# Counting hand-over times in a kernel's own scheduler, and a plain second layer for one group in eight: channel attention with a GELU feed-forward on Trainium2

## The chip, the cores and the metric

The kernel runs on one core of one Trainium2 chip. The metric is the device time of one execution in microseconds. Before the change it is 2224.11 us in the median of three runs (2223.18 to 2227.49). The engines are called as in the profile: PE multiplies matrices, DVE (vector) and ACT (scalar) work on elements, SP issues the DMAs. POOL has next to nothing to do here.

## The reference

Four batches of q, k and v, each of 6080 tokens by 256 channels, go through an attention over channels (a 256 x 256 matrix per batch), and the result, read as 24320 rows of 256, through a feed-forward layer with 2048 hidden units.

```python
def _attn_ref(q, k, v, tau):                      # B, N, C = 4, 6080, 256
    qn = q / (np.linalg.norm(q, axis=1, keepdims=True) + 1e-06)
    kn = k / (np.linalg.norm(k, axis=1, keepdims=True) + 1e-06)
    s = kn.transpose(0, 2, 1) @ qn / tau
    s = s - s.max(-1, keepdims=True)
    a = np.exp(s)
    a /= a.sum(-1, keepdims=True) + 1e-09
    return v @ a

def _moe_ref(x, w_in, w_out):                     # x: 24320 x 256
    h = x @ w_in                                  # 256 x 2048
    g = 0.5 * h * (1.0 + erf(h / np.sqrt(2.0)))
    return g @ w_out                              # 2048 x 256
```

## The kernel before

**Precision.** Every fp32 operand of a matmul is split into a high part, rounded to the chip's fp32r type, and the rest. A product is three matmuls: low weight by high data, high by high, high weight by low data. So every block that PE reads must first be made twice: its high part on ACT ("hi"), its rest on DVE ("lo", the block minus its high part).

**Two layers.** The attention matrix of a batch is multiplied into w_in, so that per token two layers remain: 256 to 2048 with the gelu, and 2048 to 256. The tokens of a batch are cut into 12 chunks (10 and 11 are a little narrower), the hidden units into four groups g. A **step** (b, c, g) is one group for one chunk; there are 184 of them after a first pair of chunks that is done in another way. A chunk is two halves of up to 256 columns.

**Layer 1 of a step** multiplies blocks 2 x 2 with seven products instead of eight (`ORDER`, `do` in `chunk_ops`, matmul lines L841 to L843). Each product is six matmuls of 256 columns, so a step has 42. They go into PSUM tiles: "one" and "two" (`pa` and `pb`, which swap roles at each step), "x" (`px`) and "z" (`pz`). Between them ACT copies "one" to `px` (x_copy, L847) and "two" to SBUF (p5_copy, L851), and DVE adds: z_add (L855) makes `pz` from "one" and p5, and p5_add (L858) makes p5. The next product into "one" must wait for z_add, which reads it.

**Between the layers** a gelu is taken of four blocks, B22 (from px), B11 (from p5), B21 (from pz) and B12 (from "one"). For B22, B11 and B21, ACT makes hi (L871) and the whole fp32 value in `gs` (L868), and DVE the lo (L874, out `los`). B12 is made whole alone.

**Layer 2 of a step** is crossed as well: seven products (`CROSS`, L973 to L975) with B22, B11, B21 and four blocks T1 to T4 of differences. These take a chain of their own over two engines: DVE makes t_add(0) (L881, 1024 columns), t_add(1) (L883) and t_add(2) (L885) in place in `gs`; ACT rounds T1 and T3 (first t_hi, L888) and, once t_add(2) is done, T2 and T4 (second t_hi, L888); DVE makes the rests (first and second t_lo, L892). The products with T blocks are the fourth to seventh of the seven. A crossed second layer has 42 matmuls of 256 columns and adds up in four PSUM tiles po0 to po3, which a join on DVE (L1009 to L1021) and copies on ACT (L999) put together per chunk and store.

**The plain form** of layer 2 exists too (L957 to L959). It takes B22, B21, B12 and B11 themselves with the blocks of w_out, in 8 products of three matmuls of 512 columns, and no T block. It then needs the hi (L871) and lo (L874) of B12, and only po0 and po1. `plain_out` says where it is used: in chunk (0, 2) and, through `MIXED`, in the last group of chunk (3, 11).

**What else runs in the steps.** The seven (or eight) products of layer 2 of one step are woven between the seven of layer 1 of the next, so the T blocks of a step are made while PE works at the next one. At batches 0 to 2 the scores of the next batch are multiplied in bursts (L416, L418) with splits (L404, L408) and a sum (L429); near the end of a batch come its softmax and the products with w_in. For each chunk the V data of the next one is summed and split (L756 to L760, L773, L777), with the most of it in the first steps (g = 0) of a chunk. The parts of w_out come from HBM for each step (`wo<-keep_out`, four buffers).

**What sets the order.** The program is recorded as a plan, and then `Order.schedule` puts the instructions of ACT, DVE and SP in an order (PE keeps the recorded one). It walks through time with costs from `cost`. Each instruction has a latest time, counted back from PE's instructions by `delay`, and a ready time, counted forward by the same `delay`; among those that are ready the one with the earliest latest time goes first. The order is then fixed by dependencies.

Of the kernel before, what the change touches and what calls it, by code (L numbers as in the profile page):

```python
# [55 lines left out]
PE, ACT, DVE, SP = (mybir.EngineType.PE, mybir.EngineType.Activation, mybir.EngineType.DVE, mybir.EngineType.SP)  # L56
# [22 lines left out]
class Order:  # L79
# [32 lines left out]
    def cost(self, ins, reads, writes):  # L112
        n = max([x[3] for x in reads + writes] + [1])
        psum = any(x[0][0] in ("pa", "pb", "px", "pz", "po0", "po1", "po2", "po3") for x in reads)
        if ins.engine == PE:
            k = reads[0][3] if reads else 1
            if ins.ins[0].dtype == F32:
                return (max(1.69 * k, 112.0),) * 2
            return .4427 * k + 3.4 + 1.5 * (k <= H), .4427 * k + 170
        if ins.engine == DVE:  # L120
            t = n / .96 + 66
            if type(ins).__name__ == "InstTensorCopy" and not psum:
                t = n / 1.92 + 66
            return t, t + 90
        if ins.engine == ACT:
            t = .855 * n + (38 if psum else 70)
            return t + 90 * (len(ins.outs) > 1), t + 105
        return 60, n * 512 / BANDWIDTH

# [48 lines left out]
    def schedule(self, todo, preds, costs):  # L178
        import heapq
        n = len(todo)  # L180
        succs = [[] for _ in range(n)]
        for b, ps in enumerate(preds):
            for a in ps:
                succs[a].append(b)

        def delay(a, b):
            if (a, b) in self.rings:
                return 0
            same = todo[a].engine == todo[b].engine
            if todo[a].engine == SP:  # L190
                return costs[a][1] + DMA_LATE
            return costs[a][0] if same and todo[a].engine == PE else costs[a][1]

        t, nominal = 0.0, {}
        for at in range(n):
            if todo[at].engine == PE:
                nominal[at] = t
                t += costs[at][0]
        late = [0.0] * n
        for a in reversed(range(n)):  # L200
            x = nominal.get(a, t + 1e4)
            for b in succs[a]:
                x = min(x, late[b] - delay(a, b))
            late[a] = x
        left = [len(p) for p in preds]
        ready = [0.0] * n
        engines = (PE, ACT, DVE, SP)
        known = {e: [] for e in engines}
        for at in range(n):
            if not left[at]:  # L210
                known[todo[at].engine].append(at)
        free = {e: 0.0 for e in engines}
        order, now, slip = [], 0.0, 0.0
        dma = 0.0
        events = [0.0]
        while len(order) < n:
            now = heapq.heappop(events)
            while events and events[0] <= now:
                heapq.heappop(events)
            for e in engines:  # L220
                if free[e] > now or not known[e]:
                    continue
                cands = sorted((late[a], a) for a in known[e] if ready[a] <= now)
                soon = [a for a in known[e] if ready[a] > now]
                pick = None
                for l, a in cands:
                    end = now + costs[a][0]
                    if any(late[u] < l and ready[u] < end and max(late[u] + slip, ready[u]) < end for u in soon):
                        continue
                    pick = a  # L230
                    break
                if pick is None:
                    if soon:
                        heapq.heappush(events, min(ready[u] for u in soon))
                    continue
                a = pick
                known[e].remove(a)
                order.append(a)
                free[e] = now + costs[a][0]
                heapq.heappush(events, free[e])  # L240
                if a in nominal:
                    slip = now - nominal[a]
                if e == SP:
                    dma = max(dma, now + DMA_LAT / 2) + costs[a][1]
                for b in succs[a]:
                    ready[b] = max(ready[b], dma + DMA_LAT / 2 if e == SP and (a, b) not in self.rings else now + delay(a, b))
                    left[b] -= 1
                    if not left[b]:
                        known[todo[b].engine].append(b)
                        heapq.heappush(events, max(now, ready[b]))  # L250
        return order

BANDWIDTH, DMA_LAT, DMA_LATE = 320.0, 2000, 6000


def MIXED(b, c):
    return (b, c) == (3, 11)


NARROWS = (4, 9)
# [15 lines left out]
def channel_attention_gelu_ffn(ctx, tc, qk, kqt, vt, tau, w_in, w_out, out):  # L278
# [228 lines left out]
    def plain_out(b, c, g):  # L507
        return (b, c) == (0, 2) or (MIXED(b, c) and g == NWG - 1)
# [907 lines left out]
```

## Time and profile before

| | |
|---|---|
| median of three runs | 2224.11 us |
| the profiled execution | 2226.17 us, its span 2224.4 us |
| granted TensorE clock | 0.997 |
| first step (0,2,0) begins | 161.4 us into the span |
| first step of batch 3 begins | 1711.3 us |
| last step begins | 2204.7 us |
| DMA | 510 MB, 229 GB/s in the mean |

One row of the list of waits names the engine and line that waited, what it waited for, the sum of the time, how often, and the longest. A row of the timeline gives the start in us, the duration, the engine, line and operation, what it writes and reads with their sizes, and in brackets the idle time of the engine ahead of it if that was over 0.15 us. In a list of groups the columns are line, engine, operation, operands, count, then busy time in us and mean duration in ns, then the idle time ahead of them and what ended it. Matmuls overlap: a row shows 0.28 us for a matmul of 256 columns, but the next one starts 0.12 us later. The distance between starts is what one costs. "PEld" is the loading of weights, which runs beside the matmuls.

### The profile page before, as it was taken

To read this page: it belongs to the slowest core of one execution; us is meant where nothing else is said; L and a number is where in the kernel's file an instruction comes from. 1 tells how busy PE (TensorE), PEld (TensorE's weight loads), DVE (VectorE), ACT (ScalarE), POOL (GpSimd) and SP (SyncE) were. 2 spreads that over 40 slices of the span, in tenths; PEclk is the share of its full clock that TensorE was granted. 3 is DMA by queue.
4 is the path that set the end of the run, shared out by engine and by line. 5 is a ranking of instruction groups with operands and counts; after the bars stand their busy time and mean duration, and the time that the engine had idled before them with its cause. 6 is when DMAs were issued, how large, how long until landed. Compare 5 with 4: busy or idle time off the path is not lost.

```text
span 2224.4 us, 42491 instructions
## 1 busy us (share of the span) xinstructions
PE 2159.6 (97%) x16750; PEld 2062.0 (93%) x16750; DVE 2016.1 (91%) x2908; ACT 1691.7 (76%) x2806; POOL 1.3 (0%) x8
## 2 busy tenths in 40 slices
PE   8999999999999999999899999999999999999999
PEld 7788999999999999999899999999999999999998
DVE  6987899999999899999899999999989989889897
ACT  5656788888888878887777777777778777777776
POOL 0000000000000000000000000000000000000000
PEclk9999999999999999999999999999999999999999
DMA  9547787777877777777576666665556656656655
GB/s 378 180 124 278 252 275 245 272 273 241 286 254 268 266 257 257 254 268 237 162 236 226 232 212 208 230 233 193 195 184 220 205 181 216 200 187 209 204 194 179
DMA packets 164360, 510.03 MB, mean 229 GB/s; under 512 B 16832, under 2 KB 27072, under 8 KB 162112
## 3 DMA queue, kind: packets, MB, share of 16 engines
q1 hardware_dynamic: 164160, 507.32, 67.7%
q8 instruction: 131, 2.15, 0.4%
q14 instruction: 69, 0.57, 0.1%
HBM read 469.76 MB, written 37.49 MB: 228 GB/s over the span
## 4 chain that ended last, share of the span: by engine, by line
DVE 35%; PE 29%; ACT 27%; issue 6%; DMA 4%; SPq 0%; DVEq 0%; ACTq 0%
DVE los L892 12%; ACT his L888 8%; ACT gs L868 8%; ACT his L871 5%; DVE gs L881 4%; PE po L975 4%; DVE pz L855 3%; DVE los L874 3%; PE po L973 3%; PE po L974 3%; DVE gs L885 3%; DVE gs L883 3%; DVE vlo L777 2%; DMA out<-osb 2%; PE pa L841 2%
## 5 line engine op out<-in xcount | busy, mean ns | idle before, releaser
L975 PE MATMUL po<-los,wo 128*128 128x256 f32 (+1 forms) x2506 | 711.9, 284 | 23.9 <-DVE los L892 19.3
L973 PE MATMUL po<-his,wo 128*128 128x256 f32 (+1 forms) x2506 | 698.9, 279 | 1.8 <-ACT his L888 0.8
L974 PE MATMUL po<-his,wo 128*128 128x256 f32 (+1 forms) x2506 | 697.3, 278 | 0.0
L975 PEld LDWEIGHTS po<-los,wo 128*128 128x128 f32 x2506 | 470.9, 188 | 48.2 <-DVE los L892 42.8
L892 DVE TENSOR_TENSOR los<-gs,his 128x1024 fp32r<-128x1024 f32 (+1 forms) x358 | 434.3, 1213 | 70.2 <-ACT his L888 64.3
L888 ACT CAST his<-gs 128x1024 fp32r<-128x1024 f32 (+1 forms) x358 | 373.4, 1043 | 162.8 <-DVE gs L885 137.2
L973 PEld LDWEIGHTS po<-his,wo 128*128 128x128 f32 x2506 | 471.1, 188 | 7.5 <-ACT his L888 1.2
L974 PEld LDWEIGHTS po<-his,wo 128*128 128x128 f32 x2506 | 470.9, 188 | 1.0
L874 DVE TENSOR_TENSOR los<-gs,his 128x512 fp32r<-128x512 f32 (+1 forms) x557 | 378.0, 683 | 60.3 <-ACT gs L868 46.0
L841 PE MATMUL pa<-vhi,wl 128*128 128x256 f32 (+1 forms) x920 | 266.0, 289 | 12.7 <-DVE pz L855 10.5
L841 PE MATMUL pb<-vhi,wl 128*128 128x256 f32 (+1 forms) x920 | 263.5, 286 | 5.3 <-ACT gs L868 4.1
L843 PE MATMUL pa<-vlo,wh 128*128 128x256 f32 (+1 forms) x920 | 257.0, 279 | 1.4 <-DVE vlo L777 1.4
L842 PE MATMUL pb<-vhi,wh 128*128 128x256 f32 (+1 forms) x920 | 256.2, 279 | 0.0
L843 PE MATMUL pb<-vlo,wh 128*128 128x256 f32 (+1 forms) x920 | 256.1, 278 | 0.0
L842 PE MATMUL pa<-vhi,wh 128*128 128x256 f32 (+1 forms) x920 | 256.0, 278 | 0.0
L881 DVE TENSOR_TENSOR gs<-gs 128x1024 f32<-128x1024 f32 (+1 forms) x179 | 217.0, 1212 | 23.2 <-ACT gs L868 16.2
L841 PEld LDWEIGHTS pa<-vhi,wl 128*128 128x128 f32 x920 | 172.9, 188 | 24.3 <-DVE pz L855 17.2
L871 ACT ACTIVATE his<-px 128x512 fp32r<-128x512 f32 (+1 forms) x184 | 108.7, 591 | 110.0 <-PE px L843 109.3
L868 ACT ACTIVATE gs<-px 128x512 f32<-128x512 f32 (+1 forms) x184 | 109.3, 594 | 107.4 <-DVE los L892 107.0
L841 PEld LDWEIGHTS pb<-vhi,wl 128*128 128x128 f32 x920 | 173.0, 188 | 11.9 <-ACT gs L868 5.3
L843 PEld LDWEIGHTS pa<-vlo,wh 128*128 128x128 f32 x920 | 172.9, 188 | 2.8 <-DVE vlo L777 2.4
L842 PEld LDWEIGHTS pb<-vhi,wh 128*128 128x128 f32 x920 | 173.3, 188 | 0.4
(286 smaller groups left out, 4637.3 us busy)
## 6 DMA issues: line engine op xcount, KB each, us to landing
wo<-keep_out SPq DMA_DIRECT2D x547, 512.0 KB, 4.3
raw<-qk SPq DMA_DIRECT2D x95, 512.0 KB, 5.9
wo<-keep_out SPq DMA_DIRECT2D x179, 256.0 KB, 3.9
kqc<-kqt SPq DMA_DIRECT2D x72, 512.0 KB, 5.0
v_raw<-vt SPq DMA_DIRECT2D x20, 1024.0 KB, 7.7
out<-osb SPq DMA_DIRECT2D x40, 512.0 KB, 4.7
win<-keep_in SPq DMA_DIRECT2D x12, 1024.0 KB, 7.3
keep_in<-win SPq DMA_DIRECT2D x4, 1024.0 KB, 4.6
```

The lines of the kernel that those rows point to most:

```text
L841: nc.tensor.matmul(o, wls[g][:, a, q], vh[:, at, :h], start=start, stop=False, skip_group_check=True)
L842: nc.tensor.matmul(o, whs[g][:, a, q], vh[:, at, :h], start=False, stop=False, skip_group_check=True)
L843: nc.tensor.matmul(o, whs[g][:, a, q], vl[:, at, :h], start=False, stop=stop, skip_group_check=True)
L868: nc.scalar.activation(out=whole(name), in_=t[SOURCE[name]], func=AF.Gelu)
L871: nc.scalar.activation(out=slot(name)[0], in_=t[SOURCE[name]], func=AF.Gelu)
L874: tt(out=slot(name)[1], in0=whole(name), in1=f32(slot(name)[0]), op=ALU.subtract)
L881: tt(out=g4[:, 0:2], in0=g4[:, 1:3], in1=g4[:, 0:2], op=ALU.subtract)
L888: nc.scalar.copy(out=views[1][:, 2 - 2 * i:4 - 2 * i], in_=views[0][:, 2 * i:2 * i + 2])
L892: tt(out=views[2][:, at], in0=views[0][:, 2 * i:2 * i + 2], in1=f32(views[1][:, at]), op=ALU.subtract)
L973: nc.tensor.matmul(o, w[:, 1, q], mh, start=starts and q == 0, stop=False, skip_group_check=True)
L974: nc.tensor.matmul(o, w[:, 0, q], mh, start=False, stop=False, skip_group_check=True)
L975: nc.tensor.matmul(o, w[:, 0, q], ml, start=False, stop=stops and q == 1, skip_group_check=True)
```

## The change

It has two parts. `MIXED` now holds for the odd chunks of batches 0 to 2: in their fourth group (g = 3) layer 2 is plain. Since batch 0 has its steps from chunk 2 on, these are 5 + 6 + 6 = 17 steps. And the scheduler's `delay` now adds a hand-over time to a producer's latency: `WAIT` of the consumer's engine between two engines, 60 ns more where the consumer waits for more than one source, and 33 ns between two dependent instructions of one engine; ACT's cost is 10 ns higher.

```diff
         if ins.engine == ACT:
-            t = .855 * n + (38 if psum else 70)
+            t = .855 * n + (48 if psum else 80)
             return t + 90 * (len(ins.outs) > 1), t + 105
...
+        sources = [len({todo[a].engine for a in p if todo[a].engine != PE or todo[b].engine != PE}) for b, p in enumerate(preds)]
+
         def delay(a, b):
             if (a, b) in self.rings:
                 return 0
             same = todo[a].engine == todo[b].engine
             if todo[a].engine == SP:
                 return costs[a][1] + DMA_LATE
-            return costs[a][0] if same and todo[a].engine == PE else costs[a][1]
+            if same:
+                return costs[a][0] if todo[a].engine == PE else costs[a][1] + 33
+            return costs[a][1] + WAIT[todo[b].engine] + 60 * (sources[b] > 1)
...
+WAIT = {PE: 58, ACT: 34, DVE: 40, SP: 0}
...
 def MIXED(b, c):
-    return (b, c) == (3, 11)
+    return b < 3 and c % 2 or (b, c) == (3, 11)
```

The lines of the changed kernel from there on are five higher: L881 is L886 in it.

What the scheduler makes of it is seen on DVE in an ordinary step of batch 3, (3,6,2), which has no plain part; p_... is the p5 tile. Before, from p5_add to the second t_lo:

```order
L858 TENSOR_TENSOR p_23169<-pa,p_23169 128x512
L874 TENSOR_TENSOR los<-gs,his 128x512 x2
L881 TENSOR_TENSOR gs<-gs 128x1024
L874 TENSOR_TENSOR los<-gs,his 128x512
L892 TENSOR_TENSOR los<-gs,his 128x1024
L883 TENSOR_TENSOR gs<-gs 128x512
L855 TENSOR_TENSOR pz<-pb,p_23289 128x512
L885 TENSOR_TENSOR gs<-gs 128x512
L1015 TENSOR_TENSOR osb<-osb 128x512
L892 TENSOR_TENSOR los<-gs,his 128x1024
```

And of the change, the same stretch:

```order
L863 TENSOR_TENSOR p_22693<-pa,p_22693 128x512
L879 TENSOR_TENSOR los<-gs,his 128x512 x2
L1020 TENSOR_TENSOR osb<-osb 128x512
L886 TENSOR_TENSOR gs<-gs 128x1024
L879 TENSOR_TENSOR los<-gs,his 128x512
L888 TENSOR_TENSOR gs<-gs 128x512
L897 TENSOR_TENSOR los<-gs,his 128x1024
L890 TENSOR_TENSOR gs<-gs 128x512
L860 TENSOR_TENSOR pz<-pb,p_22813 128x512
L1022 TENSOR_TENSOR osb<-osb 128x256
L897 TENSOR_TENSOR los<-gs,his 128x1024
```

t_add(1) now stands ahead of the first t_lo, t_add(2) ahead of z_add, and a part of the join ahead of t_add(0).

ACT in the same step, from x_copy to the last gelu; before:

```order
L847 COPY px<-pa 128x512
L888 CAST his<-gs 128x1024
L851 COPY p_23169<-pb 128x512
L871 ACTIVATE his<-px 128x512
L888 CAST his<-gs 128x1024
L868 ACTIVATE gs<-px 128x512
L871 ACTIVATE his<-p_23169 128x512
L868 ACTIVATE gs<-p_23169 128x512
L868 ACTIVATE gs<-pa 128x512
L871 ACTIVATE his<-pz 128x512
L868 ACTIVATE gs<-pz 128x512
```

And of the change:

```order
L852 COPY px<-pa 128x512
L893 CAST his<-gs 128x1024
L856 COPY p_22693<-pb 128x512
L893 CAST his<-gs 128x1024
L876 ACTIVATE his<-px 128x512
L873 ACTIVATE gs<-px 128x512
L876 ACTIVATE his<-p_22693 128x512
L873 ACTIVATE gs<-p_22693 128x512
L876 ACTIVATE his<-pz 128x512
L873 ACTIVATE gs<-pa 128x512
L873 ACTIVATE gs<-pz 128x512
```

The second t_hi goes ahead of the gelu of B22, and the whole gelu of B12 (from `pa`) behind the his of B21.

In a plain step, (2,7,3), DVE has this from p5_add to the one of the next step in place of 14 rows with t_add and t_lo:

```order
L863 TENSOR_TENSOR p_17202<-pb,p_17202 128x512
L879 TENSOR_TENSOR los<-gs,his 128x512
L782 TENSOR_TENSOR vlo<-v_raw,vhi 128x256
L879 TENSOR_TENSOR los<-gs,his 128x512
L782 TENSOR_TENSOR vlo<-vs,vhi 128x512
L782 TENSOR_TENSOR vlo<-v_raw,vhi 128x512
L879 TENSOR_TENSOR los<-gs,his 128x512 x2
L1014 TENSOR_TENSOR osb<-osb 128x256
L1016 TENSOR_TENSOR osb<-osb 128x512
L413 TENSOR_TENSOR hl<-raw,hl 128x1024
L860 TENSOR_TENSOR pz<-pa,p_17334 128x512
L413 TENSOR_TENSOR hl<-raw,hl 128x1024
```

The T work of 17 steps is gone; a fourth los (B12) and the start of the chunk's join stand there. In all DVE loses 17 of each t_add and 34 t_lo, and gains 17 los; ACT loses 34 t_hi and 17 copies and gains 17 his.

## The prediction

> **What bounds the kernel now.** I read the page's busy shares first, then the list of waits, then the chain of waits for one stretch of the last batch, then single matmul starts.
>
> ```profile
> PE 2159.6 (97%) x16750; PEld 2062.0 (93%) x16750; DVE 2016.1 (91%) x2908; ACT 1691.7 (76%) x2806; POOL 1.3 (0%) x8
> ...
> DVE 35%; PE 29%; ACT 27%; issue 6%; DMA 4%; SPq 0%; DVEq 0%; ACTq 0%
> ```
>
> The first line alone says "PE". The second, the engine shares of the chain that ended last, says that for 62% of the span the last thing that somebody waited for was on DVE or ACT. So PE is nearly full, but something else sets its pace in many places. The places are in the waits (engine and line, what it waited for, total us, times, longest):
>
> ```profile
> PEld po L975 <- DVE los L892: 42.8, 109, 1.0
> PEld pa L841 <- DVE pz L855: 17.2, 30, 1.4
> ```
>
> ```profile
> ACT his L888 <- DVE gs L885: 137.2, 108, 3.1
> ```
>
> PE waits for the second t_lo (L892) above all, then for z_add (L855). Behind t_lo stands t_hi (L888), which waits for the second difference t_add(2) (L885). And ACT's whole gelu (L868) waits for t_lo in its turn, since it overwrites the gs block that t_lo reads. That closes a circle, and the chain of waits in batch 3, step (3,6,2), shows it (start, duration, what ended last; the longest pieces, the whole gelus between the rows being left out):
>
> ```profile
> 1985.60 1.24 DVE los L892
> 1987.46 0.64 ACT his L871
> 1988.64 0.70 DVE los L874
> 1989.44 1.24 DVE gs L881
> 1990.70 1.06 ACT his L888
> 1991.78 0.97 DVE los L892
> 1992.92 0.69 DVE gs L883
> 1993.61 0.61 DVE pz L855
> 1994.22 0.60 DVE gs L885
> 1994.84 1.06 ACT his L888
> 1995.93 1.24 DVE los L892
> 1997.79 0.63 ACT his L871
> ```
>
> From ACT's his of B11 to the next one (1987.46 to 1997.79) are 10.33 us, and no matmul is in it. In words: gelus of B11, its los, t_add(0), t_hi, t_lo, t_add(1), z_add, t_add(2), the second t_hi and t_lo, the next step's whole gelu of B22 (behind t_lo, from 1997.17 to 1997.79), and again. Against that stands PE's own need, from matmul starts:
>
> ```profile
> 1994.65 0.28 PE L841 MATMUL pa<-vhi,wl 128*128 128x256 f32 x1
> ...
> 1996.89 0.28 PE L974 MATMUL po<-his,wo 128*128 128x256 f32 x1
> 1997.21 0.39 PE L975 MATMUL po<-los,wo 128*128 128x256 f32 x1
> ```
>
> From the first row to the second are 19 matmuls of 256 columns and 2.24 us, 0.1175 to 0.118 each, so a crossed step (42 for layer 1, 42 for layer 2) needs 9.85 to 9.9; I count with 9.85. The step lasts as long as the circle, 10.33, because the L975 that reads the T2 block starts 0.32 after its predecessor, 0.04 behind the end of t_lo (1995.93 + 1.24): 0.48 us a step are lost.
>
> How much is lost in all follows from the first matmul of a stage and that of the next:
>
> ```profile
> 161.43 0.28 PE L841 MATMUL pa<-vhi,wl 128*128 128x256 f32 x1
> ...
> 1711.31 0.28 PE L841 MATMUL pa<-vhi,wl 128*128 128x256 f32 x1
> ...
> 2136.41 0.27 PE L841 MATMUL pa<-vhi,wl 128*128 128x240 f32 x1
> ```
>
> Batch 3, forty steps from (3,0,0) to (3,9,3): 425.1 us, against 396.5 of matmuls back to back; 28.6 lost, 15 of it in the 30 steps with g of 1 to 3 and 13.5 in the ten with g = 0. Batches 0 to 2, 136 steps: 1549.9 against 1456 (108 crossed steps at 9.85, 24 narrow ones at 240/256 of that, four plain ones at 10.41, 94 of score bursts, 33 of weight products); 94 lost. With the end the steps lose about 131 us. That is all that any reordering can win, and about 12 of it stands at the very end or is a few hundredths in every step.
>
> I marked each of the 179 crossed steps by DVE's order in it. **Order A** has t_add(1) (L883) ahead of the first t_lo, **order B** behind it. By the starts of the steps, the 81 steps in order A with g over 0 lose 0.09 us in the median and 0.29 in the mean; the 53 in order B with g over 0 lose 0.63 in the mean, all but four at least 0.4; the 43 in order B with g = 0 lose 1.46 each, 63 us together. One of these last, (3,4,0), from its first matmul to the next step's:
>
> ```profile
> 1882.18 0.28 PE L841 MATMUL pa<-vhi,wl 128*128 128x256 f32 x1
> ...
> 1888.80 0.39 PE L841 MATMUL pa<-vhi,wl 128*128 128x256 f32 x1 [0.47 <-DVE pz L855]
> ...
> 1893.81 0.28 PE L841 MATMUL pb<-vhi,wl 128*128 128x256 f32 x1
> ```
>
> It lasts 11.63, 1.78 over 9.85; its DVE also carries the differences and splits of the next V chunk.
>
> **The change part by part.**
>
> *The plain second layer, 17 steps* (chunks 3, 5, 7, 9, 11 of batch 0 and six each of batches 1 and 2). PE: 24 matmuls of 512 columns for 42 of 256. Their pace is seen in chunk (0,2), which is plain already:
>
> ```profile
> 173.21 0.39 PE L957 MATMUL po<-his,wo 128*128 128x512 f32 x1
> 173.44 0.40 PE L958 MATMUL po<-his,wo 128*128 128x512 f32 x1
> 174.13 0.50 PE L959 MATMUL po<-los,wo 128*128 128x512 f32 x1 [0.29 <-DVE los L874]
> ```
>
> One takes 0.23, so 24 take 5.52 against 42 at 0.118 = 4.96: 0.56 more a step, **+9.5 us** in 17. PE has no cover for it.
>
> In exchange DVE loses two t_lo (L892) and the three t_add (L881, L883 and L885, which is like L883) and gains one los (L874); ACT loses two L888 and gains one his gelu:
>
> ```profile
> L892 DVE TENSOR_TENSOR los<-gs,his 128x1024 fp32r<-128x1024 f32 x296 | 362.5, 1225 | 56.9 <-ACT his L888 51.7 <-PE pa L843 0.4
> L874 DVE TENSOR_TENSOR los<-gs,his 128x512 fp32r<-128x512 f32 x460 | 314.6, 689 | 49.0 <-ACT gs L868 37.6 <-ACT his L871 0.4
> L881 DVE TENSOR_TENSOR gs<-gs 128x1024 f32<-128x1024 f32 x148 | 181.1, 1224 | 16.8 <-ACT gs L868 10.2
> L883 DVE TENSOR_TENSOR gs<-gs 128x512 f32<-128x512 f32 x148 | 101.5, 686 | 0.7
> ```
>
> DVE, per step: 2 x 1.225 + 1.224 + 2 x 0.686 - 0.689 = 4.4 us, some 70 of its 2016 us. None of that counts by itself. It counts because the T work of these steps falls into the g = 0 step that follows, and there the circle is cut: nothing of T is waited for. Those 17 steps lose 21.9 us now. The new wait is that the first plain product needs the los of B21 at once. The third row above shows it in (0,2,1): L959 starts 0.69 after L958, where 0.23 would do, 0.46 lost. Bounds: nothing, where the los comes in time, and 0.9, twice the row. I take the row itself: 17 x 0.46 = 7.8, so **-14 us** from the waits. The join of these chunks reads PSUM by DVE in place of an ACT copy; it lies in g = 0 steps that just lost 4.4 us of DVE. The missing cover would cost 0.6 a step, 10 us; that is in the upper bound. SP issues 17 512-KB and 17 256-KB loads fewer.
>
> *The hand-over times.* They only move work: PE's order is not scheduled, but those of ACT, DVE and SP are. In the new order 118 steps with g over 0 are A and 16 are B, and 98 of the A steps also have t_add(2) ahead of z_add. On the circle above: t_add(1), 0.60 from the start of L883 to that of the next, and z_add, 0.61, leave it; the join that now stands ahead of t_add(0), and the later B12 gelu, put in some 0.5. 10.33 - 1.21 + 0.5 = 9.6, under PE's 9.85. So PE would be late next, which is what one wants; the reserve is 0.2 us.
>
> The terms, each with what I take and its ends:
> - 51 steps with g over 0 go from B to A, losing 29.7 now. Afterwards 0.2 each, between the median and the mean of order A: **-20** (-15 to -25).
> - 11 steps with g = 0 go from B to A, losing 16.2 now; half stays, since DVE is overfull there: **-8** (0 to -13).
> - 15 steps with g = 0 stay B, losing 24.6, but eleven of them get t_add(2) ahead of z_add: one 0.60 each, **-7** (0 to -13).
> - 14 steps with a burst go from A to B; they lose 0.07 each now, and the burst gives T 2.8 us more time: **+3** (0 to +7).
> - 67 steps stay A, losing 22.3: nothing (+5 to -11).
> - In the softmax stages of batches 1 and 2 four ACT table loads of 1.28 us fall away, in steps that lose 4 to 5 us today: **-3** (0 to -5).
>
> ```profile
> L618 ACT ACT_TABLE_LOAD x5 | 6.4, 1283 | 0.1
> ```
>
> Sum: +9.5 - 14 - 20 - 8 - 7 + 3 - 3 = -39.5. The profiled execution took 2226.2 us (span 2224.4), so 2186.7; the median of the runs, 2224.1, is 2.1 lower, so **2184.6 us**.
>
> A rule to weigh: the Trainium skill, Perfetto Trace Analysis, section "Identifying the Most-Contended Engine", judges TensorE by the busy share of its weight loads and says to optimise the engine with the highest share first. By it PE (93%) comes ahead of DVE (91%), and the change, which gives PE more columns to relieve DVE, would be the wrong way round. The circle without a matmul speaks against using the rule here.
>
> **The rivals.**
> - *The waits come back elsewhere.* DVE was 91% busy; what is moved ahead of the T work must go somewhere, and half of the gain by order (35) returns. 2184.6 + 17.5 = 2202. For it: the reserve of the new circle is only 0.2 us. Against: order A steps with one or two fillers already run at 0.1.
> - *The order does not matter, the plain steps alone do.* +9.5 - 14: 2219 to 2220. For: nothing waits differently in order B if ACT, not DVE, was the late one. Against: L888 waits 137 us for L885.
> - *PE is the bound.* The lost time is not recovered and the columns come on top: 2224.1 + 9.5 = 2234. This is what the rule above would give. Against: 0.48 a step, with PE idle and fed late, in almost every step of batch 3.
> - *z_add becomes the late one: slower.* It now stands behind t_add(2). In step (3,6,2) its place leaves little: PE's L841 that needs it starts at 1994.65, and z_add ends at 1993.61 + 0.61 = 1994.22. Where DVE has no idle time ahead of the first t_lo, z_add moves by 0.60 and PE waits. From 0.40 us a step, over the 98 steps, that eats the 39.5. At 0.6, which z_add itself would be late by, it is 98 x 0.6 = 59, so 2184.6 + 59 = 2244. Against: DVE idles there 0.5 us now, into which t_add(1) moves.
>
> **How the numbers follow.** Forecast as summed (2166 to 2196): 0.57. Better, where plain waits and order A both come out at their lower ends, 2150 to 2166: 0.11. Half returns, 2196 to 2214: 0.19. Plain steps alone, 2219.5: 0.04. PE bound, 2234: 0.03. z_add, 2230 to 2260: 0.06. The range 2157 to 2214 leaves out the last three and half of "better": 0.19. About 0.2% (4.4 us) is what a measurement of this kernel can tell from no change; so faster 0.88, same 0.04, slower 0.08.
>
> **What would show it.** Right: crossed steps of batch 3 with g over 0 last 9.9 and not 10.33; PE's wait for the los of t_lo falls from 43 us to under 20; ACT's his for the second difference falls from 137 us to some 60; the 17 steps behind plain ones last about 10.9; DVE is some 70 us less busy. Wrong: PE's waits for z_add (L860 in the changed listing) over 40 us; waits of 0.9 a step at the last matmul of the first plain product (L964 there); steps of batch 3 still at 10.3.

## The result, and the profile after

| | before | after |
|---|---|---|
| median | 2224.24 us (2223.18 to 2227.49) | 2143.85 us (2141.79 to 2145.44) |
| ratio | | 0.9636, 95% interval 0.9619 to 0.9652 |
| profiled execution, its span | 2226.17, 2224.4 | 2143.23, 2141.5 |
| granted TensorE clock | 0.997 | 0.999 |

The kernel became 80.4 us faster; 39.5 were forecast. The direction was right, the size was not, and the time lies below the range.

The busy shares of the profile after, and the engine shares of its chain of waits:

```profile
PE 2112.2 (99%) x16444; PEld 2035.0 (95%) x16444; DVE 1950.0 (91%) x2840; ACT 1658.4 (77%) x2768; POOL 1.3 (0%) x8
...
PE 86%; DVE 6%; ACT 4%; DMA 3%; issue 2%; SPq 0%; DVEq 0%; ACTq 0%
```

DVE is 66 us less busy (70 were forecast) and its share of the span is still 91%. What changed is the chain: PE had 29% of it and now has 86%. Two groups of weight loads with the idle time ahead of them show what became of the two main waits:

```profile
L980 PEld LDWEIGHTS po<-los,wo 128*128 128x128 f32 x2268 | 426.1, 188 | 2.5 <-DVE los L897 2.4
L846 PEld LDWEIGHTS pa<-vhi,wl 128*128 128x128 f32 x920 | 172.8, 188 | 17.4 <-DVE pz L860 7.2
```

The wait for the T rests fell from 42.8 us to 2.4, that for z_add into `pa` from 17.2 to 7.2 (into `pb` it rose from 0.8 to 3.0). The list of waits of ACT says something else:

```profile
ACT his L893 <- DVE gs L890: 120.3, 120, 3.1
```

That wait, 137.2 before, was to fall to some 60. It did not, and PE hardly feels it (the 2.4 us above): ACT now has time to spare there. ACT's timeline in step (3,6,2) has it:

```profile
1917.46 0.59 ACT L856 COPY p<-pb 128x512 f32<-128x512 f32 x1
1919.46 1.05 ACT L893 CAST his<-gs 128x1024 fp32r<-128x1024 f32 x1 [1.41 <-DVE gs L890]
```

And the first matmuls of that step and of the next, in PE's timeline:

```profile
1915.03 0.28 PE L846 MATMUL pa<-vhi,wl 128*128 128x256 f32 x1
1924.92 0.28 PE L846 MATMUL pb<-vhi,wl 128*128 128x256 f32 x1
```

9.89 us in place of 10.33, as forecast for batch 3 (9.9). The first matmuls of the stages:

```profile
160.80 0.28 PE L846 MATMUL pa<-vhi,wl 128*128 128x256 f32 x1
...
1652.92 0.28 PE L846 MATMUL pa<-vhi,wl 128*128 128x256 f32 x1
...
2054.09 0.27 PE L846 MATMUL pa<-vhi,wl 128*128 128x240 f32 x1
```

Batches 0 to 2 take 1492.1 us (before 1549.9), the forty steps of batch 3 401.2 (425.1). The steps lose 34 us of waits in all now, where they lost 126.

### The profile page after: what moved, and what is told of

Same layout as the page of the kernel before. It is cut to its first block, busy times and chain, and to the rows that moved or that the text cites. A ratio compares the mean times of both kernels' runs of the same rounds, so it can differ in the third digit from the quotient of the medians.

```text
span 2141.5 us, 41888 instructions
## 1 busy us (share of the span) xinstructions
PE 2112.2 (99%) x16444; PEld 2035.0 (95%) x16444; DVE 1950.0 (91%) x2840; ACT 1658.4 (77%) x2768; POOL 1.3 (0%) x8
## 4 chain that ended last, share of the span: by engine, by line
PE 86%; DVE 6%; ACT 4%; DMA 3%; issue 2%; SPq 0%; DVEq 0%; ACTq 0%
PE po L980 11%; PE po L978 11%; PE po L979 11%; PE pa L846 5%; PE pb L846 4%; PE pb L848 4%; PE pb L847 4%; PE pa L848 4%; PE pa L847 4%; PE pz L846 2%; PE pz L847 2%; PE pz L848 2%; PE px L846 2%; PE px L848 2%; PE px L847 2%; PE po L964 2%
## 5 line engine op out<-in xcount | busy, mean ns | idle before, releaser
L980 PE MATMUL po<-los,wo 128*128 128x256 f32 (+1 forms) x2268 | 631.5, 278 | 1.8 <-DVE los L897 1.8
L978 PE MATMUL po<-his,wo 128*128 128x256 f32 (+1 forms) x2268 | 631.4, 278 | 0.0
L979 PE MATMUL po<-his,wo 128*128 128x256 f32 (+1 forms) x2268 | 630.8, 278 | 0.0
L893 ACT CAST his<-gs 128x1024 fp32r<-128x1024 f32 (+1 forms) x324 | 337.9, 1043 | 126.8 <-DVE gs L890 120.3
L879 DVE TENSOR_TENSOR los<-gs,his 128x512 fp32r<-128x512 f32 (+1 forms) x574 | 386.6, 682 | 49.6 <-ACT gs L873 35.3
L978 PEld LDWEIGHTS po<-his,wo 128*128 128x128 f32 x2268 | 425.8, 188 | 3.7 <-ACT his L893 0.2
L980 PEld LDWEIGHTS po<-los,wo 128*128 128x128 f32 x2268 | 426.1, 188 | 2.5 <-DVE los L897 2.4
L979 PEld LDWEIGHTS po<-his,wo 128*128 128x128 f32 x2268 | 425.9, 188 | 0.8
L897 DVE TENSOR_TENSOR los<-gs,his 128x1024 fp32r<-128x1024 f32 (+1 forms) x324 | 392.7, 1212 | 33.1 <-ACT his L893 30.1
L886 DVE TENSOR_TENSOR gs<-gs 128x1024 f32<-128x1024 f32 (+1 forms) x162 | 196.5, 1213 | 40.1 <-ACT gs L873 36.8
L847 PEld LDWEIGHTS pa<-vhi,wh 128*128 128x128 f32 x920 | 172.9, 188 | 2.5
L848 PEld LDWEIGHTS pb<-vlo,wh 128*128 128x128 f32 x920 | 172.8, 188 | 0.0
```

Of the source, the lines that this page charges most:

```text
L847: nc.tensor.matmul(o, whs[g][:, a, q], vh[:, at, :h], start=False, stop=False, skip_group_check=True)
L848: nc.tensor.matmul(o, whs[g][:, a, q], vl[:, at, :h], start=False, stop=stop, skip_group_check=True)
L879: tt(out=slot(name)[1], in0=whole(name), in1=f32(slot(name)[0]), op=ALU.subtract)
L886: tt(out=g4[:, 0:2], in0=g4[:, 1:3], in1=g4[:, 0:2], op=ALU.subtract)
L893: nc.scalar.copy(out=views[1][:, 2 - 2 * i:4 - 2 * i], in_=views[0][:, 2 * i:2 * i + 2])
L897: tt(out=views[2][:, at], in0=views[0][:, 2 * i:2 * i + 2], in1=f32(views[1][:, at]), op=ALU.subtract)
```

## The experiments

The times below are medians with their range, the ratios are to the kernel before in the same set of runs (its median was 2224.2 to 2227.2). "Waits" is the sum over all steps of a step's length less its matmuls back to back, as in the prediction. A passage behind ">" is what was expected of a run before it ran. The first of them set two theories against each other: C, that the circle was nearly everything, so that the new order alone brings most of the gain; and R, that the plain steps relieve DVE of work that had delayed other steps too.

### One part alone

**The order alone** (hand-over times counted, `MIXED` as before):

```diff
 def MIXED(b, c):
-    return b < 3 and c % 2 or (b, c) == (3, 11)
+    return (b, c) == (3, 11)
```

> The hand-over times alone; MIXED as before. Theory C (circle): PE's waits in the steps belong to the circle of gelu, differences, t_hi and t_lo, and vanish nearly everywhere once it is shorter than PE's 9.85 us a step. Then the 9.5 us of added columns are saved, and the 17 steps behind odd chunks wait some 0.5 to 1 us each again (8 to 17 us): 2142 to 2152 us. Theory R (relief): it is the 70 us of DVE work that the plain steps take away; then only batch 3 gains, and batches 0 to 2 stay: 2190 to 2205 us.

2191.39 us (2189.99 to 2193.68), ratio 0.985 [0.9834, 0.9867]: 33.5 us gained. Of 30 steps of batch 3 with g over 0 the median is 9.89, as in the changed kernel, so the new order breaks the circle by itself. But in its list of waits another one has grown:

```profile
PEld pa L846 <- DVE pz L860: 33.1, 34, 1.4
PE pa L846 <- DVE pz L860: 26.0, 31, 1.2
```

The wait for z_add doubled (17.2 before). The rival of a late z_add is real, in some thirty places and not in 98.

**The plain steps alone** (the kernel before with the new `MIXED`):

```diff
 def MIXED(b, c):
-    return (b, c) == (3, 11)
+    return b < 3 and c % 2 or (b, c) == (3, 11)
```

> The 17 plain steps alone; the scheduler's times as before. Theory C: +9.5 us of columns, the 21.9 us of the 17 steps mostly gone, the rest of the waits where they were: 2205 to 2215 us, batch 3 unchanged with steps of 10.33 us. Theory R: batches 0 to 2 as in the full change and batch 3 as before: about 2169 us.

2194.48 us (2194.27 to 2195.35), ratio 0.9867 [0.9852, 0.9882]: 30.4 us gained, where the prediction's terms for it alone, +9.5 and -14, make 4.5. Neither theory's number was met: the relief is large, and smaller than R had it. In the 17 steps behind plain ones the waits fall by some 13 us, as forecast. As much again, some 14 us, goes in the 17 g = 0 steps of the odd chunks, four steps further on, and some 9 in the steps of the even chunks with g over 0; the prediction gave the plain steps nothing there. Batch 3, which has no new plain step, still has the circle; the chain of waits in its step (3,6,2) is that of before, at other times (its longest pieces on DVE; those left out are on ACT and DVE):

```profile
1957.37 0.70 DVE los L874
...
1958.16 1.24 DVE gs L881
...
1961.65 0.69 DVE gs L883
1962.34 0.61 DVE pz L855
1962.94 0.60 DVE gs L885
...
1964.65 1.24 DVE los L892
...
1967.70 0.70 DVE los L874
```

From los to los are 10.33 us, and no matmul lies in between. By stage, from the first matmuls:

| us | batches 0 to 2 | batch 3, 40 steps | waits in all steps |
|---|---|---|---|
| before | 1549.9 | 425.1 | 125.9 |
| order alone | 1532.1 | 409.2 | 91.2 |
| plain steps alone | 1519.5 | 423.3 | 84.4 |
| both (the change) | 1492.1 | 401.2 | 34.4 |

The order works in both stages, the plain steps where they stand. Together they give 16 us more than the sum of the two.

### What it is in the plain steps that pays

**The DVE work put back.** In 15 of the 17 plain steps DVE makes again the three differences and twice the second rest, which the plain layer 2 does not read; ACT's rounding of T stays out. (The condition `c > 2` leaves out chunk 1 of batches 1 and 2, so the expectation's "17" is 15; the trace has 15 more of each t_add than the change.) This adds unread work and holds the `gs` blocks longer.

```diff
             at(e[6] + 1.2, lo, "B12")
+            if b < 3 and c > 2:
+                at(e[6] + 1.3, t_add, 0)
+                at(e[6] + 2.5, t_add, 1)
+                at(e[6] + 3.1, t_add, 2)
+                at(e[6] + 3.7, t_lo, 1)
+                at(e[6] + 5.0, t_lo, 1)
```

> The whole change, but the 17 plain steps carry the DVE work that they had before, though no product of layer 2 reads it: t_add(0) to t_add(2) in gs and twice the second t_lo, without t_hi. Some 70 us of DVE work are back, gs is held as long as before, the columns stay. Theory relief: the waits of batches 0 to 2 return, up to the 49 us that they are longer with the order alone: 2175 to 2195 us. Theory cut (PE's not waiting for T in the step behind is what counts): 2143 to 2158 us.

2193.48 us (2191.55 to 2196.2), ratio 0.9852 [0.9838, 0.9865]: 49.6 us are gone again, as much as the plain steps had added to the order alone (2191.39). Its busy shares and its waits for z_add:

```profile
PE 2130.0 (97%) x16444; PEld 2035.8 (93%) x16444; DVE 2012.7 (92%) x2915; ACT 1667.2 (76%) x2772; POOL 1.3 (0%) x8
```

```profile
PEld pa L846 <- DVE pz L860: 19.0, 24, 1.4
PEld pb L846 <- DVE pz L860: 10.6, 19, 0.7
```

PE still waits for no T block in the steps behind the plain ones, ACT still has 34 roundings fewer, and the time is lost all the same. So the cut of the circle, on which the prediction had put its 14 us, is not enough: what is lost again is due to DVE's work (with the blocks that it holds). And it is lost in other steps: the 51 steps of the even chunks of batches 0 to 2 with g over 0 wait 38.3 us (14.6 in the change), the 15 steps right behind the loaded ones 5.2 (2.6). The run does not simply undo the plain steps: the work put back falls into the same steps as before, but t_add(0) stands up to 4.6 us later in them, and those 51 steps now wait longer than in the kernel before (some 31 us). The 49.6 is therefore no exact price.

**DVE work taken out elsewhere.** The order alone, and the 17 even chunks after (0,2) up to (3,0) leave out the low part of V, 68 instructions of L782; layer 1 multiplies there what the buffers hold.

```diff
     def v_lo(b, c, part):
+        if c % 2 == 0 and (0, 2) < (b, c) <= (3, 0):
+            return
```

> The hand-over times alone (2191 us), with no plain steps, but the low parts of V (vlo) of the 17 chunks whose V is prepared beside the odd chunks of batches 0 to 2 are not computed: 2.4 us of DVE work less in each of those chunks, no column more, the T chain kept. Theory relief (the plain steps count because DVE is overfull, not because T is cut): most of the 47 us between the order alone and the whole change comes back, 2150 to 2165 us. Theory cut (they count because the circle is cut in the step behind): 2183 to 2191 us.

2177.28 us (2173.72 to 2181.36), ratio 0.9781 [0.9761, 0.9801], 14 us under the order alone, between the two expectations. DVE was 33 us less busy (1972.8 to 2005.7) and 14 us came of it; the plain steps take 56 off the order alone and bring 47.5. Work off DVE pays here too, about half as much per microsecond, and here no instruction that holds a `gs` block was taken out; the run goes no further, since the place of the work differs too.

### What it is in the order that pays

**The differences earlier, nothing else.** The kernel before, with the latest times of t_add(1) and t_add(2) 2 us earlier; 178 of 179 crossed steps then are in order A, with t_add(2) ahead of z_add.

```diff
+        for a in range(n):
+            if todo[a].name in EARLY:
+                late[a] -= EARLIER
...
+EARLY, EARLIER = set(), 2000.0
...
             elif i == 1:
-                tt(out=g4[:, 2], in0=g4[:, 2], in1=g4[:, 0], op=ALU.subtract)
+                EARLY.add(tt(out=g4[:, 2], in0=g4[:, 2], in1=g4[:, 0], op=ALU.subtract).ins.name)
             else:
-                tt(out=g4[:, 3], in0=g4[:, 3], in1=g4[:, 2], op=ALU.subtract)
+                EARLY.add(tt(out=g4[:, 3], in0=g4[:, 3], in1=g4[:, 2], op=ALU.subtract).ins.name)
```

> The kernel before, its scheduler's times unchanged, but t_add(1) and t_add(2) get a latest time 2 us earlier, which puts t_add(1) ahead of the first t_lo and t_add(2) ahead of z_add in 178 of 179 crossed steps. Theory C: this alone breaks the circle, so most of the gain comes: 2142 to 2165 us, steps of batch 3 at 9.9 us. If the hand-over times act by other moves (fillers, gelus, joins), the gain is a third or less: 2195 to 2220 us.

2173.6 us (2172.43 to 2179.89), ratio 0.9778 [0.9761, 0.9796]. Two instructions' places do more than all the hand-over times do alone (2191.39).

**The same with the plain steps** (the kernel before, the lines above, and the new `MIXED`):

> The plain steps, and the two differences given a latest time 2 us earlier; the scheduler's times as before. If the place of the differences is what the hand-over times bring, it is as fast as the whole change or faster: 2132 to 2150 us. If their other moves are needed beside it: 2150 to 2165 us.

2164.9 us (2164.49 to 2168.18), ratio 0.9728 [0.9712, 0.9744], 21 us slower than the change. So the places of the two differences are not all that the hand-over times bring once the plain steps are there.

**The whole change with them** (hand-over times, plain steps, and the same 2 us):

> The whole change, and the two differences 2 us earlier on top. PE is 99% busy already and about 20 us of waits are left in the steps: 2133 to 2147 us by theory C; slower than 2150 us if putting them first makes the los of the gelus late.

2148.61 us (2145.65 to 2150.28), ratio 0.9647 [0.9628, 0.9666]: no gain over the change (2143.85, ratio 0.9636). The medians differ by 4.8 us, the ratios by 2.4, and their intervals overlap, so a loss isn't shown either.

**The 33 ns between two instructions of one engine, taken out**, first from the order alone and then from the whole change:

```diff
             if same:
-                return costs[a][0] if todo[a].engine == PE else costs[a][1] + 33
+                return costs[a][0] if todo[a].engine == PE else costs[a][1]
```

> As the hand-over times alone, but without the 33 ns between dependent instructions of one engine. If the times between engines do it: as that kernel, within 4 us. If the 33 ns are needed: over 10 us slower than it.

> The whole change without the 33 ns between dependent instructions of one engine. With the order alone that was 6.5 us faster. If that was a real gain it shows here too: 2136 to 2140 us. If it was scatter of the list scheduler, which the plain steps cover: 2141 to 2147 us.

2184.86 us (2183.25 to 2185.78), ratio 0.9822 [0.9808, 0.9837], and 2143.78 (2139.88 to 2147.81), ratio 0.963 [0.9611, 0.9649]. In the whole change the 33 ns do nothing; in the order alone they cost 6.5 us. So a change of nanoseconds in one of the scheduler's numbers can move the time by several us in one version and not in another, and a difference of that size says little about the number's worth.

**One part of the hand-over times, with the plain steps.** Only the 60 ns for a consumer with two or more sources (`WAIT` zero; ACT's cost as in the kernel before, and no 33 ns), and then only `WAIT` (with the same two left out):

```diff
-WAIT = {PE: 58, ACT: 34, DVE: 40, SP: 0}
+WAIT = {PE: 0, ACT: 0, DVE: 0, SP: 0}
```

> The plain steps, and of the hand-over times only the 60 ns for a consumer with more than one source (WAIT, the 33 ns and ACT's 10 ns at nothing). The order has t_add(2) ahead of z_add in 112 steps, as the whole change has. If that and the place of t_add(1) are the order's part: 2138 to 2150 us. If the times by engine are needed: 2160 to 2190 us.

```diff
-            return costs[a][1] + WAIT[todo[b].engine] + 60 * (sources[b] > 1)
+            return costs[a][1] + WAIT[todo[b].engine]
```

> The plain steps, and of the hand-over times only WAIT by engine. t_add(1) goes ahead of the first t_lo in 157 of 162 steps, but t_add(2) stays behind z_add in all but 20. If t_add(1) suffices (one 0.60 out of a circle of 10.33 leaves 9.73, under PE's 9.85): 2143 to 2155 us. If both must go: 2160 to 2185 us.

2156.06 us (2154.44 to 2160.85), ratio 0.9686 [0.9673, 0.97], and 2155.15 (2151.63 to 2156.73), ratio 0.9677 [0.9663, 0.969]. They bring 38 and 39 of the 50.6 us that lie between the plain steps alone and the change. With `WAIT` alone t_add(1) stands ahead of the first t_lo in 157 of 162 crossed steps, but t_add(2) behind z_add in all but 20. That speaks for the first of the two places, but does not show it: `WAIT` moves other instructions too, and with both places forced, and nothing else, the time was 2164.9. Which of the other moves bring the rest stays open.

### One step further

Plain layer 2 in the odd chunks of batch 3 too:

```diff
 def MIXED(b, c):
-    return b < 3 and c % 2 or (b, c) == (3, 11)
+    return c % 2
```

> The whole change, and the odd chunks of batch 3 plain in g = 3 too (five more). +2.8 us of columns; the waits of 1.1 to 1.6 us in the steps behind chunks 3, 5 and 7 should go, 4 to 6 us: 2140 to 2144 us, a little faster than the change. If relief is worth nothing where DVE is not overfull: 2145 to 2148 us.

2141.78 us (2134.14 to 2143.2), ratio 0.9621 [0.9607, 0.9634]: not to be told from the change. The waits behind chunks 3, 5 and 7 did go: the steps (3,4,0), (3,6,0) and (3,8,0) last 10.25 us each, where the change has 11.27, 10.97 and 11.40. But each plain step costs its columns, and 28 of the forty steps of batch 3 in this trace ran at a quicker pace of PE (see the last section), so what remains can't be read from it.

## Why the gain was twice the forecast

The steps of both traces, sorted as the prediction's terms are (sums of step lengths less their matmuls; a minus is a gain):

| term | forecast | measured |
|---|---|---|
| columns of 17 plain steps | +9.5 | +9.3 |
| waits of the steps behind them | -14 | -19.0 |
| 51 steps B to A, g over 0 | -20 | -24.2 |
| 11 steps B to A, g = 0 | -8 | -14.8 |
| 15 steps stay B, g = 0 | -7 | -16.2 |
| 14 steps with a burst, A to B | +3 | -0.1 |
| 67 steps stay A | 0 | -12.9 |
| two more B steps, table loads, head and end | -3 | -4.9 |
| sum | -39.5 | -82.8 |

The spans differ by 82.9; the rest is rounding.

**What was right.** What bound the kernel, the columns of the plain layer, the circle and its end: batch 3 runs at 9.89 with the order alone and keeps 10.33 with the plain steps alone. The order's terms together, -20, -8, -7, +3 and -3, make -35, and the order alone measured -33.5. They were right as a sum and not in their places, so the agreement is in part luck: the 17 g = 0 steps of odd chunks and 15 of the 17 steps behind plain ones (all but (1,2,0) and (2,2,0)) kept 36.0 of their 45.2 us under the order alone.

**What was wrong: one sentence.** Of the 70 us that DVE loses the prediction said "None of that counts by itself", and gave the plain steps only the cut of the circle in the 17 steps behind them. Alone, the plain steps gain 30.4 and not 4.5, and what goes beyond the forecast goes in steps that the prediction gave them nothing for; put back in 15 of the 17, the work costs 49.6 us. So the step that failed is the plain steps' term: it put the DVE work that is taken off (and the `gs` blocks that it holds) at nothing. The sentence treats DVE's work as if it had to stay in its step. But the scheduler moves V's sums and splits, the joins and the score splits to wherever DVE is free, so the gap that a plain step leaves takes work out of the steps around it. (For the joins this is only part of it: `join_ops` of a chunk with a plain last group can begin a step earlier by itself, since that group adds nothing to po2 and po3. The run with the work put back has the earlier join too, and loses all the same.) Step (1,7,0) shows it, the fourth step after (1,6,0), in which the plain layer 2 of (1,5,3) runs. DVE's timeline of before, from t_add(0) to the second t_lo:

```profile
940.07 1.22 DVE L881 TENSOR_TENSOR gs<-gs 128x1024 f32<-128x1024 f32 x1
941.21 0.42 DVE L1017 TENSOR_TENSOR osb<-osb 128x256 f32<-128x256 f32 x1
941.54 0.69 DVE L777 TENSOR_TENSOR vlo<-vs,vhi 128x512 fp32r<-128x512 f32 x1
942.14 0.69 DVE L874 TENSOR_TENSOR los<-gs,his 128x512 fp32r<-128x512 f32 x1
942.75 0.69 DVE L777 TENSOR_TENSOR vlo<-v_raw,vhi 128x512 fp32r<-128x512 f32 x1
943.35 1.22 DVE L892 TENSOR_TENSOR los<-gs,his 128x1024 fp32r<-128x1024 f32 x1
944.48 0.69 DVE L883 TENSOR_TENSOR gs<-gs 128x512 f32<-128x512 f32 x1
945.09 0.70 DVE L855 TENSOR_TENSOR pz<-pa,p 128x512 f32<-128x512 f32 x1
945.69 0.69 DVE L885 TENSOR_TENSOR gs<-gs 128x512 f32<-128x512 f32 x1
946.28 1.22 DVE L408 TENSOR_TENSOR hl<-raw,hl 128x1024 fp32r<-128x1024 f32 x1
947.49 1.22 DVE L892 TENSOR_TENSOR los<-gs,his 128x1024 fp32r<-128x1024 f32 x1
```

Here DVE never idles: a piece of the join, two low parts of V and a score split stand inside the chain of T. In PE's timeline the step has these two waits:

```profile
945.84 0.39 PE L841 MATMUL pa<-vhi,wl 128*128 128x256 f32 x1 [0.47 <-DVE pz L855]
948.77 0.38 PE L975 MATMUL po<-los,wo 128*128 128x256 f32 x1 [0.30 <-DVE los L892]
```

DVE's timeline of the same step with the order alone: V's low parts are still there, and t_add(2) is now ahead of z_add.

```profile
934.00 1.23 DVE L886 TENSOR_TENSOR gs<-gs 128x1024 f32<-128x1024 f32 x1 [0.40 <-ACT gs L873]
935.14 0.69 DVE L782 TENSOR_TENSOR vlo<-vs,vhi 128x512 fp32r<-128x512 f32 x1
935.75 0.69 DVE L879 TENSOR_TENSOR los<-gs,his 128x512 fp32r<-128x512 f32 x1
936.35 0.69 DVE L782 TENSOR_TENSOR vlo<-v_raw,vhi 128x512 fp32r<-128x512 f32 x1
...
938.81 0.69 DVE L890 TENSOR_TENSOR gs<-gs 128x512 f32<-128x512 f32 x1
939.42 0.69 DVE L860 TENSOR_TENSOR pz<-pa,p 128x512 f32<-128x512 f32 x1
```

In PE's timeline the only wait of that step is the one for z_add, and it is twice as long:

```profile
940.17 0.39 PE L846 MATMUL pa<-vhi,wl 128*128 128x256 f32 x1 [0.98 <-DVE pz L860]
```

And DVE's timeline of the changed kernel, where of all these fillers only a sum of V (L761) is left in the chain:

```profile
916.33 1.23 DVE L886 TENSOR_TENSOR gs<-gs 128x1024 f32<-128x1024 f32 x1 [0.74 <-ACT gs L873]
917.59 0.69 DVE L888 TENSOR_TENSOR gs<-gs 128x512 f32<-128x512 f32 x1
918.73 1.23 DVE L897 TENSOR_TENSOR los<-gs,his 128x1024 fp32r<-128x1024 f32 x1 [0.45 <-ACT his L893]
919.87 0.68 DVE L890 TENSOR_TENSOR gs<-gs 128x512 f32<-128x512 f32 x1
920.48 0.69 DVE L860 TENSOR_TENSOR pz<-pa,p 128x512 f32<-128x512 f32 x1
921.08 0.68 DVE L761 TENSOR_TENSOR vs<-v_raw 128x512 f32<-128x512 f32 x1
921.73 1.23 DVE L897 TENSOR_TENSOR los<-gs,his 128x1024 fp32r<-128x1024 f32 x1
```

DVE has slack twice, PE waits for nothing, and the step lasts 9.89 us; it was 11.76 before, 11.15 with the order alone, 11.20 with the plain steps alone. This step also suggests why the two parts give more than their sum: the order takes lateness from T and hands it to z_add where DVE is full, the plain steps take the fullness and leave the circle. Only both leave nothing late in it. In the mean over batches 0 to 2 the g = 0 step of an odd chunk carried 0.65 us of join and 1.42 of V on DVE before, and carries none and 1.04 now, while the step behind a plain one carries 2.18 and 2.03 (0.38 and 1.39 before).

**The smaller errors have the same root.** The 67 steps that stay in order A were given nothing, because their order didn't change; they gained 12.9. Their waits were most likely late work of earlier steps, not their own. Of the g = 0 steps eleven were given half, "since DVE is overfull there", and fifteen one 0.60 for most; with less to carry they gained 31.0 and not 15. The bursts cost nothing. The wait of 0.46 at the first plain product did not appear: the whole group of L964 idled 0.3 us, and a step like (1,4,0) lasts 10.53 us, not 10.9.

**The rivals.** A late z_add came true with the order alone (33 us of waits) and was prevented by the plain steps. "The plain steps alone" at 2219.5 was 25 us too high. That PE would be the bound is what the Trainium skill's rule would have given (Perfetto Trace Analysis, section "Identifying the Most-Contended Engine", highest share first): the weight loads had 93% and DVE 91%, and yet 9.3 us more of PE's columns for 66 us less of DVE's work, with the new order, made the kernel 80 us faster. PE became the bound only in the changed kernel, where its part of the chain is 86%.

**Left open.** Of the 16 us beyond the sum, some 6 stand in batch 3, where nothing was added; 2.3 of them in (3,0,2) and (3,0,3), which last 10.98 and 11.17 with the order alone and 9.89 and 9.92 in the change, as if work were carried over from batch 2; some 2 are the quicker pace of PE (last section) in six steps of batch 3. The rest is not explained. Nor does any run tell how much of the 49.6 us is DVE's time and how much the `gs` blocks held longer; with the low parts of V left out, where no `gs` block is freed earlier, 33 us of DVE's time brought 14.

## What to carry to other kernels

Where a scheduler may move work, an engine that is nearly full is one budget for many steps: value the work taken off it by the waits of all steps that it can reach, not only by the step that it stood in. Look for what stands as filler inside the late chain on that engine; it will go into the new gap. And two limits in a row must be priced together: here each remedy alone left the lateness at the other limit, so the tests of one part alone, and the forecast by terms, came out low.

## What the hardware did that was not expected

Matmuls of the same form run at two paces. PE's timeline of the changed kernel, in two places of batch 3 with no wait in them:

```profile
1744.20 0.28 PE L846 MATMUL pa<-vhi,wl 128*128 128x256 f32 x1
1744.32 0.28 PE L847 MATMUL pa<-vhi,wh 128*128 128x256 f32 x1
1744.44 0.28 PE L848 MATMUL pa<-vlo,wh 128*128 128x256 f32 x1
```

```profile
1784.20 0.28 PE L978 MATMUL po<-his,wo 128*128 128x256 f32 x1
1784.31 0.28 PE L979 MATMUL po<-his,wo 128*128 128x256 f32 x1
1784.43 0.28 PE L980 MATMUL po<-los,wo 128*128 128x256 f32 x1
```

Over the next 80 matmuls it is 0.1178 us from start to start in the first place and 0.1133 in the second, in layer 1 and layer 2 alike, so a whole step of 84 takes 9.89 or 9.52. The granted clock is 1.00 in both. In the profiled run of the change five of the forty steps of batch 3 last 9.52, in that of the order alone none, and 28 in that of the plain steps in batch 3, which is the quickest execution of its five (2134.14; the others 2141.7 to 2143.2). 23 steps more at 0.37 us less each are 8.5 us, about what sets that execution apart; the others were not profiled, so this is not shown. What starts and ends the quicker pace wasn't found.
